# Two-layer recurrent attention: new order times for the nodes inside a tile and near the layer ends, and other reload counts

## The chip, the cores and the metric

The kernel runs on one core of a Trainium2 chip. The metric is the device time of one execution in microseconds: 1611.34 us before, the median of three runs (1610.76 to 1618.56).

## The reference

The input x has 2048 rows of 512 bf16 numbers. Two blocks, A and B, are applied in turn, and the pair twice over with the same weights ("two layers"):

```python
    x = x + _A_ref(_layernorm(x, axis=-1), A_mem0, A_Wq, A_Wk, A_Wv, A_Wo, A_seg_len)
    x = x + _B_ref(_layernorm(x, axis=-1), B_wqkv, B_wo)
```

and the same two lines again. A is attention in 64 segments of 32 rows, one after the other. Each segment puts 8 memory rows in front of its 32 rows, projects these 40 rows to queries, keys and values of 32 heads of 128, takes a masked softmax over the 40 rows and projects back with Wo. The first 8 rows of the outcome are the memory of the next segment; the others are the output rows:

```python
            h = jnp.concatenate([mem, xs], axis=1)
            q = jnp.einsum('btd,dhe->bhte', h, Wq)
...
            o = jnp.einsum('bhte,hed->btd', o, Wo)
            mem = o[:, :M, :].copy()
```

So the 64 segments of a layer are a chain: no K, Q or V of a segment's memory rows can be projected before the segment before is out. B is linear attention over all 2048 rows with 32 heads of 16: phi of keys and queries, the sums kv and z over all rows, then a division and a projection. B's sums need all rows of A, and the second layer's A needs B's outcome.

## The kernel before, in words

All four A weights (4 MB each) stay in SBUF. The kernel walks 64 steps a layer, one per segment; four steps share a tile of 128 rows, so there are 16 tiles a layer, 32 in all. In the text, tile 16 is the first of layer 1, and step 25 is the second step of the seventh tile of a layer. Most matmuls use 32 columns of TensorE, four side by side on the four column groups ("x4" in the timeline).

The work of a step is recorded as nodes by `_Prog.add` (L649): each has a function, what it reads and writes, and a key (layer, step, name, number). Nodes of one step, by name:

- kq0, kq1: project K and Q of half of the heads (L1138, matmuls at L1157 with a weight load and L1053 without), then evict (L937 on ScalarE, L938 on VectorE) and transpose (L1175). v: project the values.
- mem0, mem1: attention of the memory rows, half of the heads each (L1237): scores (L1258, L1264), Exp (L1275), two mask multiplies on VectorE (L1285), the sum matmuls (L1065), Ln and Exp for the reciprocal (L1294, L1296), the product with the values (L1065), a multiply (L1307).
- out: eight matmuls with Wo (L1400), two evictions. next: picks the memory rows (L1424), whose eviction writes the next step's input. Then the next kq0 can start. This loop is the recurrence.
- x: attention of the 32 new rows (L1312), which the next step's out takes up, so it fills TensorE while the recurrence waits.
- res: adds the output rows to y (L1435) and moves them by GpSimd's DMAs (L953) into the rows' place in dx; each fourth step also the "left" rows (the last 8 rows of each segment) with eight DMAs, and then the row add x += dx (L1474). Two DMAs of every step and eight of each fourth have about 0.5 us each on GpSimd.
- bi (b_in, L1545): once a tile, B's first half for the rows that are done: bn_stats (L1097), bn_aggr, two small ScalarE steps, the normalising row (L1103), transposes (L1111), an eviction, and the products for K, V and Q of B with phi. In layer 0 these are full-width 128-column matmuls (`whole`, L1049); in layer 1 they are 32-column ones (`tiled`, L1057 to L1066).
- prep, left0, left1, leftv, lefts: normalisation and projections for the next tile. In layer 1, bo (`b_out`, L1642) gives the next tile's rows from layer 0's B. At the layers' ends: bm (`b_mid`), bl (last `b_out`), spin (matmuls that compute nothing, L1069).

**What sets the order.** The order is written into the program: `schedule()` (L698) gives each node a time by `when()` (L579), sorts all nodes by it, and each engine issues its nodes in this order. The same sort picks the eight PSUM banks, and a letter behind the time picks the engine of an eviction that either engine could do ("a" ScalarE, "v" VectorE):

```python
    own = _OWN.get((layer, step, name), ())
    if k < len(own) and own[k] is not None:
        t, eng = own[k]
    else:
        n, o, table = _PERIOD[layer]
        t, eng = table[name][step % 4][k]
        t += o + n * (step // 4)
```

The times serve only as sort keys; no engine waits for a clock. OWN (L187) has own times for nodes of the first and last steps of a layer; all other tiles take theirs from PERIOD (L19), one table of four steps for each layer, repeated every 44,811 (layer 0) or 47,442 (layer 1). So all tiles 3 to 13 of layer 0 have one order, and tiles 18 to 29 another. `finalize()` (L735) then works out which semaphore waits are needed; a later order may need more or fewer of them.

FRESH (L1130) and the third number of some SPIN entries (L1068) say how many weight loads are issued that the matmul could do without: in the value projection the second part repeats the same weights as the first, and the first `(FRESH + g) // 4` of its matmuls in step g of a tile load them again all the same. PEld in the profile is these loads and all others.

In a steady tile of layer 0, TensorE's program has 1536 matmuls, 1269 loads and 11 waits, 2816 instructions; in layer 1, 1664, 1398 and 10, 3072. Both are multiples of 256.

Of the kernel before, what the change touches and what calls it, by code (L numbers as in the profile page):

```python
# [19 lines left out]
    0: (44811, 12575, {  # L20
# [4 lines left out]
            0: '13110 13623 13859 13975 15568a 16359 16126a 16539',  # L25
            1: '25411 26062 26347 26877 27130v 27885 26918a 27828',
            2: '37244 37328 37706 38196 38237v 39335 38569a 38761',
            3: '46334 46412 46663 46947 47259a 47283 47040v 47538',
        },
        'kq1': {  # L30
            0: '13353 14813 15519 15623 16502a 16799 17302a 18507',
            1: '27317 27535 27794 27900 28953a 29844 28921a 29499',
            2: '38227 38383 38402 39545 39901a 40319 39946v 40115',
            3: '46952 47061 47181 47186 47861a 48996 48101v 48997',
        },
        'v': {
            0: '17492 17691 18869 18940 20511a 21964v',
            1: '27961 28639 28667 29491 30125a 31273a',
            2: '40039 40052 40430 40622 42339v 43144a',
            3: '47627 48767 49623 50288 50598a 52349v',  # L40
        },
        'ql': {
            0: '15578v 15115v',
            1: '17461v 26861v',
            2: '38451a 37269v',
            3: '46898a 43786v',
        },
        'mem0': {
            0: '16546 16829 17294 17722 17785 18016 18583 21138 21803 22217',
            1: '28936 29458 29710 29934 30400 30773 31025 31760 31385 33035',  # L50
            2: '39583 39632 40375 40378 41630 42130 42645 42774 42871 42913',
            3: '47989 48336 48416 49298 49214 51527 52026 52221 51908 52564',
        },
        'mem1': {
            0: '18585 18761 20500 21528 21516 21884 21908 22571 22489 22811',
            1: '29565 29979 30292 31154 31139 32247 33262 33833 33659 33946',
            2: '40730 40943 42442 42507 42731 42909 43420 43710 43574 44077',
            3: '49723 49762 49955 51484 51262 51932 52684 52852 52517 53969',
        },
        'out': {  # L60
            0: '22634 22646 22723 22911 23010 23518 23814 23993 24202a 24185a',
            1: '34034 34103 34175 34442 34686 35087 35287 35328 35887a 35715a',
            2: '43410 43727 43813 44632 44797 44941 45160 45262 45405a 45620a',
            3: '52679 52859 53388 53737 54082 54749 54845 55140 55959a 56101a',
        },
        'next': {
            0: '24849 24871 25273a',
            1: '36147 36448 37154a',
            2: '45618 45634 45742v',
            3: '56912 57244 57340a',  # L70
        },
        'res': {
            0: '24394 25027 25086 14340 14734 14783 16191 16354 17003 17419 18155 19251a 19806a 19967 21627 22615 21487 23944 21934 20248 20479 24471 28189',
            1: '37622 42461 40621',
            2: '46643 49596 51348',
            3: '56350 59264 64311',
        },
        'bi': {
            2: '28195 28607 29504 29672 29909 30351 32430 30430v 31577 31585 31911 32074 37050 37706 38060 64732 66227 69129 69420 69916a 70219 69486 80150 71185 64667 66976 69466 69753 70445 70925 71377 76228',
# [8 lines left out]
            2: '1858 14289 22297 27278 30922 32637 34676v 41100a 36482v 36690v 34762v',  # L88
        },
        'left0': {  # L90
            2: '35441 35565 36649 37230 38164v 45925 41246a 44765',
        },
        'left1': {
            2: '42823 42990 45458 45659 46883a 56541 49015a 57506',
# [1643 lines left out]
```

## Time and profile before

| what | value |
|---|---|
| median of 3 runs | 1611.34 us |
| the profiled execution | 1611.15 us |
| its span | 1609.4 us |
| around the span | 1.75 us |
| granted TensorE clock, mean | 0.998 |
| VectorE evictions (L938) | 576 at 545 ns |
| ScalarE evictions (L937, arena) | 1140 at 488 ns |
| DMAs of GpSimd into dx | 504, issued in 511 ns each, landing after 1.6 and 1.9 us |
| GpSimd busy | 326.8 us |

The profile's engines are PE (TensorE's matmuls), PEld (its weight loads, which overlap PE), DVE (VectorE), ACT (ScalarE), POOL (GpSimd). Matmuls are piped and their ends are modelled, so PE counts as busy in some gaps too. The start takes 43.6 us, of which the first 36 wait for the weights: the transfer of Wv lands 33.8 us after its issue. The last tile of layer 0, with B's middle behind it, takes 71.7 us (747.66 to 819.38), the first two of layer 1 take 44.6 and 49.6, the tile before the last 48.1 (1485.5 to 1533.6).

A row of the waits reads: the engine and line that waited, behind the arrow what it waited for, then the total us, how often, and the longest. A row of the timeline reads: start in us from the span's start, duration, engine, line, operation, output and inputs with their shapes, how many in a row were put together, and in brackets the wait ahead of it.

### The profile page before, as it was taken

How to read it: one execution, taken by the hardware profiler on the slowest of the kernel's cores; microseconds unless marked ns; L12 is line 12 of the kernel's file. 1: busy time of each engine (PE TensorE's matmuls, PEld its weight loads, DVE VectorE, ACT ScalarE, POOL GpSimd, SP SyncE). 2: the span in 40 equal slices, each digit the busy share in tenths (PEclk: the TensorE clock that was granted, in tenths of full speed). 3: DMA queues.
4: the chain of work that ended last, by engine and by line, in shares of the span. 5: the costliest groups of instructions: out<-in, count | busy, mean ns of one | idle time of the engine just before them, and what ended most of it. 6: DMA issues, size and time to landing. Idle time of an engine off the chain costs nothing.

```text
span 1609.4 us, 104163 instructions
## 1 busy us (share of the span) xinstructions
PE 1544.0 (96%) x52074; PEld 882.0 (55%) x43376; DVE 1221.6 (76%) x3899; ACT 1100.0 (68%) x3178; POOL 326.8 (20%) x660
## 2 busy tenths in 40 slices
PE   5899999999999999999999999999999999999997
PEld 1455555555555555555545655556556555555554
DVE  3777777887777787777677778777787877877777
ACT  1567776776776776776467777777777777776665
POOL 2022221122222112222201221222221222221120
PEclk9999999999999999999999999999999999999999
DMA  9300000000000000000000000000000000000013
GB/s 381 104 14 16 14 17 10 16 17 17 17 14 17 10 17 16 17 17 17 25 8 11 17 20 20 20 14 17 21 17 20 21 20 11 21 17 22 24 43 130
DMA packets 35079, 50.96 MB, mean 32 GB/s; under 512 B 13624, under 2 KB 28784, under 8 KB 33104
## 3 DMA queue, kind: packets, MB, share of 16 engines
q0 software_dynamic: 21744, 19.78, 4.3%
q1 hardware_dynamic: 12736, 24.38, 4.1%
q8 instruction: 374, 6.13, 1.6%
q14 instruction: 65, 0.53, 0.1%
q10 hardware_dynamic: 160, 0.14, 0.0%
HBM read 29.63 MB, written 10.49 MB: 25 GB/s over the span
## 4 chain that ended last, share of the span: by engine, by line
PE 85%; DVE 5%; ACT 5%; DMA 2%; issue 1%; POOL 0%; DVEq 0%; SPq 0%
PE pb L1157 27%; PE pb L1053 22%; PE pb L1400 17%; PE pb L1065 11%; ACT arena_sb L937 3%; PE pb L1049 3%; PE pb L1424 2%; DMA Wq_sb<-in_A_Wq_dram 2%; PE pb L1258 2%; DVE arena_sb L938 1%; PE pb L1338 1%; PE pb L1111 1%; DVE st_sb L1097 1%; DMA dx_sb<-y_sb 1%; DVE Wq_sb L1679 1%
## 5 line engine op out<-in xcount | busy, mean ns | idle before, releaser
L937 ACT ACTIVATE arena_sb<-pb 128x512 bf16<-128x512 f32 (+5 forms) x1140 | 521.0, 488 | 273.5 <-PE pb L1053 165.2
L953 POOL DMA_DIRECT2D dx_sb<-y_sb x504 | 254.6, 511 | 1047.7 <-DVE y_sb L1435 822.3
L1157 PE MATMUL pb<-Wk_sb,arena_sb 128*32 128x512 bf16 x4096 | 408.5, 379 | 3.0 <-DVE arena_sb L938 1.4
L1053 PE MATMUL pb<-Wq_sb,arena_sb 128*32 128x512 bf16 x4096 | 408.1, 379 | 0.0
L938 DVE CAST arena_sb<-pb 128x512 bf16<-128x512 f32 (+3 forms) x576 | 311.5, 545 | 110.9 <-PE pb L1053 57.9
L1400 PE MATMUL pb<-Wo_sb,arena_sb 128*32 128x256 bf16 x10368 | 345.3, 273 | 4.3 <-DVE arena_sb L1307 1.7
L1065 PE MATMUL pb<-arena_sb 128*32 128x128 bf16 (+2 forms) x12528 | 321.7, 216 | 4.2 <-ACT arena_sb L937 1.5
L1065 PEld LDWEIGHTS pb<-arena_sb 128*32 128x32 bf16 x12528 | 227.7, 96 | 138.1 <-issue 28.5
L1175 DVE STREAM_TRANSPOSE arena_sb<-arena_sb 128x256 f32<-128x256 f32 x640 | 260.9, 429 | 42.8 <-ACT arena_sb L937 36.6
L1400 PEld LDWEIGHTS pb<-Wo_sb,arena_sb 128*32 128x32 bf16 x10368 | 263.1, 96 | 50.6 <-issue 15.7
L1157 PE MATMUL pb<-Wv_sb,arena_sb 128*32 128x512 bf16 x3248 | 279.6, 378 | 1.1 <-DVE arena_sb L938 1.1
L1157 PEld LDWEIGHTS pb<-Wk_sb,arena_sb 128*32 128x32 bf16 x4096 | 119.4, 96 | 237.5 <-issue 186.2
L1053 PE MATMUL pb<-Wv_sb,arena_sb 128*32 128x512 bf16 x1872 | 202.8, 378 | 0.0
L937 ACT ACTIVATE arena_sb<-arena_sb 32x256 bf16<-32x256 bf16 (+1 forms) x414 | 159.6, 386 | 31.3 <-DVE arena_sb L1345 21.4
L1157 PEld LDWEIGHTS pb<-Wv_sb,arena_sb 128*32 128x32 bf16 x3248 | 95.9, 96 | 73.6 <-issue 19.2
L937 ACT ACTIVATE outW_sb<-pb 128x128 fp32r<-128x128 f32 x317 | 70.3, 273 | 89.2 <-PE pb L1400 86.2
L1307 DVE TENSOR_TENSOR arena_sb<-pb,arena_sb 128x128 bf16<-128x128 f32 x252 | 73.1, 290 | 50.5 <-PE pb L1400 17.2
L1157 PE MATMUL pb<-Wq_sb,arena_sb 128*32 128x512 bf16 x1024 | 101.6, 378 | 4.5 <-DMA Wq_sb<-in_A_Wq_dram 3.4
L1275 ACT ACTIVATE arena_sb<-pb 128x192 bf16<-128x192 f32 (+1 forms) x256 | 83.9, 328 | 31.2 <-PE pb L1258 12.7
L1435 DVE TENSOR_TENSOR y_sb<-pb,outW_sb 64x256 bf16<-64x256 f32 x158 | 65.8, 417 | 47.6 <-ACT outW_sb L937 44.2
L1053 PE MATMUL pb<-Wk_sb,arena_sb 128*32 128x512 bf16 x1024 | 101.7, 378 | 0.0
L1285 DVE TENSOR_TENSOR arena_sb<-arena_sb 128x128 bf16<-128x128 bf16 x504 | 89.0, 215 | 15.9 <-ACT arena_sb L1275 14.1
(109 smaller groups left out, 1793.0 us busy)
## 6 DMA issues: line engine op xcount, KB each, us to landing
Wk_sb<-in_A_Wk_dram SPq DMA_DIRECT2D x1, 4096.0 KB, 13.2
Wq_sb<-in_A_Wq_dram SPq DMA_DIRECT2D x1, 4096.0 KB, 24.3
Wv_sb<-in_A_Wv_dram SPq DMA_DIRECT2D x1, 4096.0 KB, 33.8
Wo_sb<-in_A_Wo_dram SPq DMA_DIRECT2D x16, 256.0 KB, 7.3
xs_scratch<-x_sb POOLq DMA_DIRECT2D x32, 128.0 KB, 2.0
pq_scratch<-arena_sb POOLq DMA_DIRECT2D x32, 128.0 KB, 2.9
dx_sb<-y_sb POOLq DMA_DIRECT2D x252, 12.0 KB, 1.6
dx_sb<-y_sb POOLq DMA_DIRECT2D x252, 4.0 KB, 1.9
```

The lines of the kernel that those rows point to most:

```text
L937: return e.activation(o() if callable(o) else o, i() if callable(i) else i, ACTF.Copy)
L938: return e.tensor_copy(o() if callable(o) else o, i() if callable(i) else i)
L953: add(eng, lambda e: e.dma_start(o, i), 0.55 if eng == "pool" else 0.4, reads=reads, writes=writes, dsem="%s%d" % (kind, k), lat=lat + (0. ...
L1053: return pe.add_instruction(mybir.InstMatmult(name=nc.get_next_instruction_name(), engine=mybir.EngineType.PE, ins=[pe.lower_ap(x), pe.low ...
L1065: r = pe.matmul(o[q], w[:, q], x, start=start, stop=stop, skip_group_check=True, tile_position=(0, 32 * j))
L1157: r = pe.matmul(o, blk[:, c, :], w, start=(c == 0), stop=(c == 3), tile_position=(0, 32 * j))
L1175: add("dve", lambda v: v.transpose(dst, src(img[:, k, :].bitcast(F32))), 0.445, reads=[("img", k)], writes=[dkey])
L1275: add("act", lambda a: a.activation(PQ[:, r2, b, 0:nq], tl.f32()[:, 0:nq], ACTF.Exp, scale=SCALE), c_act(nq), tiles=[tl], writes=[("PQ", r ...
L1285: add("dve", lambda v, a=a, p_=p_, w_=w_: v.tensor_tensor(wide(Pm[:, k, a, :]), p_.unsqueeze(2).to_broadcast([128, 4, 4, 8]), w_, ALU.mult ...
L1307: add("dve", lambda v: v.tensor_tensor(oTb[:, s % NO, 16 * b:16 * b + 16, 0:8], pv.f32()[:, 0:128].rearrange("p (n q) -> p n q", q=8), Rm[ ...
L1400: r = pe.matmul(tl.f32()[32 * j:32 * j + 32, 0:256], oT[:, 4 * hh + n, :], Wo_sb[:, 8 * n + hh, 256 * d:256 * d + 256], start=(hh == 0 and ...
L1435: add("dve", lambda v: v.tensor_tensor(y_sb[0:64, k, :], tl.f32()[0:64, 0:256], outW[64:128, w, :].bitcast(F32), ALU.add), c_dve(256), rea ...
```

## The change

No arithmetic changes. Almost every number of PERIOD and OWN does, and with them the order of nodes on every engine, the PSUM banks and the engine of many evictions; the two periods stay 44,811 and 47,442. Only relative order counts, so a shift of a whole table means nothing by itself. FRESH goes from 21 and 22 to 15 and 21 reloaded weights a tile (layers 0 and 1), and three SPIN entries load more or fewer weights again. In the changed program TensorE has the same 51,113 matmuls, 89 loads fewer and 84 wait instructions more; ScalarE has 34 instructions more and VectorE 34 fewer; GpSimd and SyncE keep theirs. A steady tile of layer 0 has 1536 matmuls, 1263 loads and 17 waits; one of layer 1 has 1664, 1397 and 11: again 2816 and 3072. A core of the diff, with the mem, res and bi rows of layer 0 that the text speaks of:

```diff
 PERIOD = {
-    0: (44811, 12575, {
+    0: (44811, 18084, {
...
         'mem1': {
...
-            1: '29565 29979 30292 31154 31139 32247 33262 33833 33659 33946',
+            1: '21770 21821 23523 24566 23897 25358 25373 25412 25370 26163',
...
         'res': {
...
-            0: '24394 25027 25086 14340 14734 14783 16191 16354 17003 17419 18155 19251a 19806a 19967 21627 22615 21487 23944 21934 20248 20479 24471 28189',
+            0: '16185 19379 21611 10728 11160 11606 11854 11856 12697 12749 12840 13857a 14265a 14789 15054 16464 16352 15143 17517 17857 18390 20872 23421',
...
         'bi': {
-            2: '28195 28607 29504 29672 29909 30351 32430 30430v 31577 31585 31911 32074 37050 37706 38060 64732 66227 69129 69420 69916a 70219 69486 80150 71185 64667 66976 69466 69753 70445 70925 71377 76228',
+            2: '23702 24471 24872 24945 25865 26463 32232 29485v 33953 33965 34004 34019 37178 38888 39017 49910 50024 60490 61903 61918a 68888 62000 71533 63097 60387 66932 66971 68576 72238 74046 74055 80677',
...
-    SPIN = {(0, 0): (24, 256, 46), (1, 0): (12,), (1, 1): (22, 256, 55), (0, 2): (5,), (0, 3): (7,), (0, 4): (30, 512, 42)}
+    SPIN = {(0, 0): (24, 256, 72), (1, 0): (12,), (1, 1): (22, 256, 84), (0, 2): (5,), (0, 3): (7,), (0, 4): (30, 512, 10)}
...
-        FRESH = {0: 21, 1: 22}
+        FRESH = {0: 15, 1: 21}
```

In these rows the last number of 'res' in step 0 is the row add x += dx, and the first of 'bi' is its bn_stats; the fourth and fifth of 'mem1' are the mask multiplies of the second half and the sixth its sum matmuls.

## The prediction

> **What bounds the kernel now.** I read the page's busy rows first, then the chain that ended last, then each stage's windows, then what TensorE waits for. The first two:
>
> ```profile
> PE 1544.0 (96%) x52074; PEld 882.0 (55%) x43376; DVE 1221.6 (76%) x3899; ACT 1100.0 (68%) x3178; POOL 326.8 (20%) x660
> ...
> PE 85%; DVE 5%; ACT 5%; DMA 2%; issue 1%; POOL 0%; DVEq 0%; SPq 0%
> ```
>
> TensorE holds the end: 85% of the chain. VectorE and ScalarE are each 5%, 161 us together of a span of 1609.4. No edit here takes matmul columns away, so the question is how much of the time that is not columns the new order gives back. The windows (us, then busy us and count of PE, PEld, DVE, ACT, POOL; granted clock; DMA) are layer 0's tiles 3 to 14, tile 6, tile 7, a tile of layer 1, and the end:
>
> ```profile
> 183.37:747.66 564.29, 555.59 (x18450) 316.48 (x15280) 437.32 (x1446) 396.88 (x1161) 118.20 (x232) 1.00 0.06 16
> 323.83:370.54 46.71, 46.19 (x1535) 26.49 (x1270) 36.31 (x121) 33.23 (x98) 9.71 (x20) 1.00 0.06 15
> 370.54:418.85 48.31, 46.49 (x1534) 25.81 (x1269) 36.27 (x121) 33.06 (x98) 9.68 (x20) 1.00 0.05 15
> 1056.32:1103.87 47.55, 46.68 (x1668) 27.65 (x1398) 37.54 (x120) 34.62 (x103) 10.28 (x21) 1.00 0.07 18
> 1533.60:1609.40 75.80, 64.11 (x2050) 36.62 (x1835) 55.56 (x137) 47.17 (x117) 13.27 (x26) 0.99 0.28 92
> ```
>
> A layer-0 tile takes about 46.7 us and one of layer 1 47.55, and they repeat: 12 and 13 such tiles are 1,180 us of the 1609. "Busy" overstates TensorE, since the modelled ends of piped matmuls run on over a gap. Adding for each matmul of a tile the shortest distance from its start to the next start that the timeline shows gives 44.37 and 45.61 us. So about 2.34 us a tile of layer 0, and 1.94 in layer 1, are waits and changes between full-width and 32-column matmuls. This is all that an order can give back there: 12 x 2.34 + 13 x 1.94 = 53 us. Who is waited for:
>
> ```profile
> PE pb L1065 <- DVE arena_sb L1285: 13.4, 31, 2.5
> PE pb L1111 <- DVE arena_sb L1103: 10.9, 4, 8.9
> PE pb L1049 <- DVE arena_sb L938: 4.7, 14, 0.8
> ```
>
> Row 1 is the sum matmul of the memory rows waiting for its two mask multiplies: 9.8 of its 13.4 us lie in layer 1's steady tiles, 0.75 us each. Row 3 is layer 0's b_in waiting for the normalised rows (12 of 14 times in steady tiles). Row 2 sits where the layers start. The timeline of the first shows its making:
>
> ```profile
> 1063.12 0.42 DVE L1474 TENSOR_TENSOR x_sb<-x_sb,dx_sb 128x512 bf16<-128x512 bf16 x1
> 1063.57 0.69 DVE L1097 BATCH_NORM_STATS2 st_sb<-x_sb 128x6 f32<-128x512 bf16 x1
> 1064.18 0.34 DVE L1285 TENSOR_TENSOR arena_sb<-arena_sb 128x128 bf16<-128x128 bf16 x2
> 1064.58 0.24 PE L1065 MATMUL pb<-arena_sb,one_sb 128*32 128x128 bf16 x4 [0.60 <-DVE arena_sb L1285]
> ```
>
> The row add and bn_stats stand on VectorE between the two halves' multiplies: 1.1 us ahead of two that take 0.34, and TensorE stops 0.60.
>
> **The change part by part.** *Work.* The matmuls are the same 51,113. The reloads that go (6 and 1 a tile, L1130) hide: the K matmuls that load and the Q matmuls of the same shape that reuse weights both have a mean of 379 ns in the groups. I take 0; since PEld lies wholly beside PE, a bound is 6 x 96 ns (mean load) = 0.6 us a tile of gain if it did not, 7 in all; loads missing elsewhere can't add time. 34 evictions go from VectorE (545 ns by the L938 row) to ScalarE (488): 18 us off one, 17 onto the other, both under 80% busy, so 0 by itself; its worth is in the waits below. The work of POOL and SP keeps its count.
>
> *Layer 0's steady tiles.* For each matmul that waits on an eviction I added up, from the trace's durations, the shortest way to it from the matmul before (matmul, 0.22 us until the eviction starts, its duration, 0.055 us to the waiting matmul), and set against it the TensorE work ordered between. Where the way is longer, the tile is late by the rest. Before: b_in's first matmul (0.93 of way, 0.71 of cover) 0.21; its sums behind phi (1.09 against 0.77) 0.32; the pick of the memory rows 0.125; the second product of memory attention 0.10; out 0.09; smaller ones. Run in order, 0.85 us a tile. After, the first two have ample cover and what is left is the next step's first K/Q matmul, 0.53 against 0.285, and 0.03: 0.28. That is -0.57. The rest of the measured 1.3 us of waits, about 0.45, is queueing on the two helper engines, which I can only bound: the new order puts the row add and bn_stats between the halves' multiplies here too, as layer 1 has them, and layer 1 pays 0.6 to 0.8 for it at 0.81 of cover. Here the cover is longer; I take 0.15 more (bounds 0 and 0.8). Two more mode changes a tile (10 to 12):
>
> ```profile
> 370.90 0.23 PE L1053 MATMUL pb<-arena_sb,one_sb 128*32 128x128 bf16 x4
> 371.06 0.40 PE L1049 MATMUL pb<-arena_sb 128*128 128x128 bf16 x4
> 371.39 0.28 PE L1065 MATMUL pb<-arena_sb 128*32 128x128 bf16 x12
> ```
>
> Each group of four 32-column matmuls has 0.053 us of columns (128 of them at 2.4 a ns, the pitch of the long runs), but the full-width matmul starts 0.16 later: about 0.10 a change. [...] I take the row, since the distance is what the next matmul paid. Sum for a tile: -0.57 + 0.15 + 0.20 = -0.22, and -0.1 more because edges within 0.25 us of late fall from 30 to 19, and each such edge turns helper jitter into a stop: about -0.3 (bounds -0.8 and +0.5). Twelve tiles: **-3.6** (-9.6 to +6).
>
> *Layer 1's steady tiles.* The same sum goes from 0.76 to 0.56. K/Q 0.24 to 0.105; the sums 0.18 to 0.12; out's first product stays, 0.43 to 0.46. VectorE keeps the row add and bn_stats between the halves, so row 1 of the waits stays; moving evictions to ScalarE frees VectorE (44.0 to 40.8 us of durations a tile) and loads ScalarE (39.9 to 42.4), where a value eviction now stands ahead of the second half. I take -0.15 of the -0.20 (bounds -0.6 and +0.6): **-2** for 13 tiles. The eight small DMAs of the left rows are issued behind an add that moves about 1 us later (from -1.74 to -0.77 us of TensorE work in the step), and their reader, the row add, stays (6.18 to 6.12): slack for them falls from about 1.6 to 0.6 us, still hidden (ten issues at the 0.51 us row, plus the 1.9 us landing row).
>
> *The start.* TensorE stops until the value weights land (near 35.6 us). Before, 14.5 us of its work is ordered ahead of that; after, 16.2, and the first out stands behind 20.2 us of work instead of 23.6. About 1.7 to 3.4 are won if the first steps keep up; they run at 10.3 to 10.8 us by their own chains and can give some back. I take **-3** (-5 to +1). *Tiles 14 to 17*: waits +0.35, ten more mode changes in tile 15 (18 to 28) at 0.10: **+1.4** (0 to +4). *Tile 30 and the end*: the same sums, 8.4 to 7.0, less what queueing takes back: **-1** (-3 to +1).
>
> Sum: -3 - 3.6 + 1.4 - 2 - 1 = -8.2 on the profiled 1611.15 (1609.4 of span and 1.75 around it), which stands 0.2 under the median: **1603 us**.
>
> **The rivals.** *Nothing measurable.* Waits move rather than go: the two helpers together have 72 of 93 us filled in a tile, my ways leave out their queues, and in layer 1 queueing was larger (1.94 - 0.76 = 1.2) than what the ways explain. If queueing grows by 0.57 in layer 0 and 0.2 in layer 1, what is left is +3.1 for mode changes and -3 at the start: 1611. For it: VectorE's row add stays where it is in layer 1. *More.* If layer 0's queueing falls with the near-late edges (-0.8 a tile) and layer 1 gains 0.4: -9.6 - 5.2 - 1.6 = 1595. *Slower.* The second half's sums in layer 0 stop behind the row add and bn_stats for the whole of these two rows, 0.42 + 0.69 = 1.1 us, in place of the 0.15 that I took: a layer-0 tile is then -0.57 + 1.1 + 0.20 = +0.73, twelve 8.8. The same delay in the first steps takes the start's gain, layer 1 gives nothing, and with +1.4 and -1 this is 1620. It decides once the two rows reach VectorE less than 1.1 us before the second half's exponentials end. The DMAs are not it: tile 7's one late landing cost 1.7 us, but slack is left. *It does nothing* in layer 1: as said, that tile's worst wait is kept.
>
> **How the numbers follow.** The forecast has 0.54 (of it 0.30 under 1603.3), more gain 0.15, nothing 0.13, slower 0.18. About 0.5%, 8 us, is what a measurement of this kernel can tell from no change: faster 0.45, same 0.37, slower 0.18. The range leaves out 0.07 below and 0.09 above: 1592 to 1621. With both signs in it, the forecast's own range is 1597 to 1609.
>
> **What would show it.** In the profile after: steady layer-0 tiles of 46.4 us (right) or 47.4 (the slower rival); the wait of L1049 for L938 gone; L1065 for L1285 still about 10 us in layer 1, and under 3 in layer 0 (8 or more: the slower rival); layer-1 tiles of 47.4; the end of tile 0 some 3 us earlier; tile 15 a us longer; PEld busy down by about 9 us with no change of PE's. A wait on dx_sb in the chain, or tiles that differ from each other, would make me wrong, as would a layer-1 tile that changes by over 0.6 us.

## The result, and the profile after

The changed kernel takes 1607.62 us (median; 1604.27 to 1611.62), the kernel before, measured beside it, 1612.94. The ratio is 0.9969 with an interval of 0.9962 to 0.9975: 5.0 us, or 0.3%, faster, where 8.2 had been forecast. The kernel before was measured beside each experiment too and had medians of 1612.9 to 1617.6, so kernels are compared by their ratios to it. The two profiled executions differ by 4.0 us (1611.15 and 1607.17), their spans by 4.2.

The page after has these busy rows and this chain:

```profile
PE 1550.3 (97%) x52121; PEld 880.0 (55%) x43287; DVE 1218.7 (76%) x3865; ACT 1101.0 (69%) x3212; POOL 324.9 (20%) x660
...
PE 88%; DVE 5%; ACT 2%; DMA 2%; issue 1%; POOL 0%; SPq 0%; DVEq 0%; ACTq 0%
```

ScalarE's share of the chain falls from 5% to 2% though it has 34 instructions more, TensorE's rises from 85% to 88%: less of the chain runs through ScalarE. PEld falls by 2.0 us, not by 9. The windows of the stages, with the columns as before (the bounds are the first K/Q matmul of step 4, step 8 and step 56 of layer 0, then of steps 0, 8 and 56 of layer 1; the stretch 82.83 to 129.49 is left out):

```profile
0.00:82.83 82.83, 59.81 (x1693) 24.98 (x1270) 42.88 (x137) 31.38 (x92) 13.38 (x50) 1.00 0.63 236
129.49:688.81 559.32, 558.78 (x18484) 317.68 (x15201) 453.89 (x1458) 383.52 (x1152) 115.98 (x228) 1.00 0.06 15
688.81:801.30 112.49, 109.69 (x3379) 62.26 (x2816) 83.83 (x259) 70.54 (x194) 26.74 (x52) 1.00 0.07 21
801.30:900.32 99.02, 95.94 (x3177) 51.13 (x2598) 74.42 (x237) 65.89 (x191) 12.79 (x25) 1.00 0.05 13
900.32:1470.70 570.38, 560.05 (x19983) 331.17 (x16769) 425.68 (x1381) 435.70 (x1273) 122.68 (x240) 1.00 0.07 18
1470.70:1605.20 134.50, 120.66 (x3993) 69.20 (x3457) 102.36 (x288) 84.13 (x221) 24.06 (x47) 0.99 0.19 61
```

The same stages of the kernel before, cut at the same matmuls, and the forecast's terms:

| stage | before, us | after, us | difference | forecast |
|---|---|---|---|---|
| start to step 4 | 81.33 | 82.83 | +1.5 | -3 (start) |
| step 4 to step 8 | 46.34 | 46.66 | +0.3 | in the start |
| layer 0, steps 8 to 56 (12 tiles) | 562.87 | 559.32 | -3.55 | -3.6 |
| layer 0's last two tiles, B's middle | 116.73 | 112.49 | -4.2 | +1.4 together |
| layer 1, steps 0 to 8 | 95.22 | 99.02 | +3.8 | (tiles 14 to 17) |
| layer 1, steps 8 to 56 (12 tiles) | 571.79 | 570.38 | -1.4 | -2 |
| the rest | 135.12 | 134.50 | -0.6 | -1 |
| sum | 1609.4 | 1605.2 | -4.2 | -8.2 |

The rows of -4.2 and +3.8 belong together: the first of them has 74 matmuls fewer than before and the second 37 more, so work has moved across the mark, and what is left of both is -0.4. Tile by tile, the steady tiles of layer 0 took 46.5 to 47.2 us and now 46.36 to 46.85. Tile 7 stands out: 48.52, now 46.85. So 1.7 of the 3.55 us are one event in one tile, and the eleven others gained 0.17 on the mean. In layer 1 the tile stays at 47.5 us.

One pair of profiles is not exact for the short stages. Five kernels below begin like one of the two, so there are four profiles of the old start and three of the new. The first matmul on the value weights came anywhere from 35.5 to 37.7 us, in both. From it to step 4, the old start took 45.40 to 45.45 us and the new one 46.5 to 47.05, so this part is 1.1 to 1.6 us longer. The whole to step 4 took 81.27 to 83.11 us in the old start and 82.09 to 83.50 in the new; there the difference between the kernels is hardly larger than the scatter.

What TensorE waits for, over the whole span (engine, line, behind the arrow what came last, then total us, times, longest):

```profile
PE pb L1067 <- DVE arena_sb L1287: 12.8, 20, 2.5
PE pb L1113 <- DVE arena_sb L1105: 10.3, 3, 9.1
...
PE pb L1426 <- ACT outW_sb L939: 2.2, 7, 0.4
...
PE pb L1055 <- issue: 1.2, 1, 1.2
```

The b_in row (L1049 for L938, 4.7 us) is gone, and L1067 for L1287 is nearly the size it was. In the window of layer 0's steady tiles (176.48 to 734.95 us) the waits have no row at all; before, b_in's matmuls alone had 5.6 us there:

```profile
PE pb L1049 <- DVE arena_sb L938: 3.7, 12, 0.3
PE pb L1049 <- issue: 1.9, 12, 0.2
```

These two rows mislead. The trace of the kernel before has 465 records of L1049's matmuls for 512 weight loads, and each of these waits stands at the second matmul of a group, 0.23 us behind the load of a first one that has no record. A kernel below with the same order in layer 0 and all 512 records (the new tables in layer 1 alone) has no such row in its tiles: there the 1.9 us are no wait, and of the 3.7 only about 0.15 us a tile is one (see the gaps below). In layer 1 the row stays; its making, in the timeline:

```profile
1108.16 0.42 DVE L1476 TENSOR_TENSOR x_sb<-x_sb,dx_sb 128x512 bf16<-128x512 bf16 x1
1108.61 0.69 DVE L1099 BATCH_NORM_STATS2 st_sb<-x_sb 128x6 f32<-128x512 bf16 x1
1109.22 0.34 DVE L1287 TENSOR_TENSOR arena_sb<-arena_sb 128x128 bf16<-128x128 bf16 x2
1109.62 0.24 PE L1067 MATMUL pb<-arena_sb,one_sb 128*32 128x128 bf16 x4 [0.63 <-DVE arena_sb L1287]
```

It is the picture of before to a few hundredths. And one stop is new, in the second step; nothing that the profile shows released the matmul behind it:

```profile
50.34 0.39 PE L1159 MATMUL pb<-Wk_sb,arena_sb 128*32 128x512 bf16 x4
51.96 0.38 PE L1055 MATMUL pb<-Wq_sb,arena_sb 128*32 128x512 bf16 x4 [1.23 <-issue]
```

The change has two parts, the order and the reload counts. The forecast gave the gain to the order (small waits in layer 0's tiles) and counted the reloads at 0. The experiments set against this: that the gain is the reloads' own; that the counts have a price by where they put TensorE's instructions; that in layer 1 another engine comes late once VectorE doesn't; and that the start is lost by its own chain. The expectations use letters for theories, and the text under each says in words which reading held.

### The profile page after: what moved, and what is told of

The parts are those of the page before. It is cut to its first block, busy times and chain, and to the rows that moved or that the text cites. A ratio compares the mean times of both kernels' runs of the same rounds, so it can differ in the third digit from the quotient of the medians.

```text
span 1605.2 us, 104159 instructions
## 1 busy us (share of the span) xinstructions
PE 1550.3 (97%) x52121; PEld 880.0 (55%) x43287; DVE 1218.7 (76%) x3865; ACT 1101.0 (69%) x3212; POOL 324.9 (20%) x660
## 3 DMA queue, kind: packets, MB, share of 16 engines
q8 instruction: 374, 6.13, 1.6%
## 4 chain that ended last, share of the span: by engine, by line
PE 88%; DVE 5%; ACT 2%; DMA 2%; issue 1%; POOL 0%; SPq 0%; DVEq 0%; ACTq 0%
PE pb L1159 27%; PE pb L1055 23%; PE pb L1402 18%; PE pb L1067 11%; PE pb L1051 3%; DMA Wv_sb<-in_A_Wv_dram 2%; ACT arena_sb L939 2%; PE pb L1260 1%; PE pb L1426 1%; PE pb L1113 1%; PE pb L1340 1%; DVE st_sb L1099 1%; DVE arena_sb L940 1%; DVE arena_sb L1287 1%; DVE Wq_sb L1681 0%
## 5 line engine op out<-in xcount | busy, mean ns | idle before, releaser
L939 ACT ACTIVATE arena_sb<-pb 128x512 bf16<-128x512 f32 (+5 forms) x1234 | 556.2, 485 | 276.9 <-PE pb L1055 182.2
L940 DVE CAST arena_sb<-pb 128x512 bf16<-128x512 f32 (+3 forms) x510 | 275.7, 544 | 103.4 <-PE pb L1055 66.5
L1067 PE MATMUL pb<-arena_sb 128*32 128x128 bf16 (+2 forms) x12528 | 326.8, 216 | 5.0 <-DVE arena_sb L1606 2.0
L1067 PEld LDWEIGHTS pb<-arena_sb 128*32 128x32 bf16 x12528 | 227.2, 96 | 130.9 <-issue 39.0
L1159 PE MATMUL pb<-Wv_sb,arena_sb 128*32 128x512 bf16 x3136 | 281.0, 378 | 1.3 <-DMA Wv_sb<-in_A_Wv_dram 0.7
L1402 PEld LDWEIGHTS pb<-Wo_sb,arena_sb 128*32 128x32 bf16 x10368 | 259.1, 97 | 35.8 <-issue 9.2
L1055 PE MATMUL pb<-Wv_sb,arena_sb 128*32 128x512 bf16 x1984 | 210.3, 378 | 0.0
L939 ACT ACTIVATE arena_sb<-arena_sb 32x256 bf16<-32x256 bf16 (+1 forms) x377 | 143.2, 380 | 14.5 <-DVE arena_sb L1347 4.6
L1159 PEld LDWEIGHTS pb<-Wv_sb,arena_sb 128*32 128x32 bf16 x3136 | 90.0, 96 | 79.2 <-issue 25.1
L1287 DVE TENSOR_TENSOR arena_sb<-arena_sb 128x128 bf16<-128x128 bf16 x504 | 91.8, 216 | 29.5 <-ACT arena_sb L1277 27.7
L1277 ACT ACTIVATE arena_sb<-pb 128x192 bf16<-128x192 f32 (+1 forms) x256 | 85.0, 333 | 41.6 <-PE pb L1260 38.1
L940 DVE COPY arena_sb<-arena_sb 32x256 bf16<-32x256 bf16 (+1 forms) x391 | 79.7, 207 | 9.1
```

The costliest lines, as they stand in the source:

```text
L939: return e.activation(o() if callable(o) else o, i() if callable(i) else i, ACTF.Copy)
L940: return e.tensor_copy(o() if callable(o) else o, i() if callable(i) else i)
L1055: return pe.add_instruction(mybir.InstMatmult(name=nc.get_next_instruction_name(), engine=mybir.EngineType.PE, ins=[pe.lower_ap(x), pe.low ...
L1067: r = pe.matmul(o[q], w[:, q], x, start=start, stop=stop, skip_group_check=True, tile_position=(0, 32 * j))
L1159: r = pe.matmul(o, blk[:, c, :], w, start=(c == 0), stop=(c == 3), tile_position=(0, 32 * j))
L1277: add("act", lambda a: a.activation(PQ[:, r2, b, 0:nq], tl.f32()[:, 0:nq], ACTF.Exp, scale=SCALE), c_act(nq), tiles=[tl], writes=[("PQ", r ...
```

## The two parts of the change apart

**The new order with the old counts.** The changed kernel, with the counts of before:

```diff
-    SPIN = {(0, 0): (24, 256, 72), (1, 0): (12,), (1, 1): (22, 256, 84), (0, 2): (5,), (0, 3): (7,), (0, 4): (30, 512, 10)}
+    SPIN = {(0, 0): (24, 256, 46), (1, 0): (12,), (1, 1): (22, 256, 55), (0, 2): (5,), (0, 3): (7,), (0, 4): (30, 512, 42)}
-        FRESH = {0: 15, 1: 21}
+        FRESH = {0: 21, 1: 22}
```

> The new order with the old reload counts (21 and 22 a tile, the old SPIN entries), so a tile is no longer 2816 or 3072 instructions of TensorE. Theory A, the order carries the change and the counts nothing: the time of the changed kernel, 1607.6 within 1 us. Theory B, the counts carry it: 1611 or more.

Measured: 1664.83 us, 1.0291 [1.0269, 1.0313] of the kernel before. The second reading held, and by far more than its 1611: the counts carry it, but not by their work. The same matmuls in the same order, with 89 weight loads more, are 52 us slower than the changed kernel (1.0291 against 0.9969), 0.58 us for each load, whose mean duration is 0.096. Its waits:

```profile
PE pb L1402 <- issue: 12.6, 32, 0.9
PE pb L1067 <- issue: 11.5, 16, 2.7
...
PE pb L1159 <- issue: 8.6, 19, 1.0
PE pb L1055 <- issue: 3.9, 8, 0.9
```

"issue" says that nothing in the profile released the engine. These stops have a place, though. I numbered TensorE's instructions (matmuls, loads and waits) in program order, each load just ahead of its matmul. All 77 waits that the profile puts down to "issue", 37.1 us together, stand in front of an instruction whose number leaves 193 or 194 when divided by 256. The page has a row that fits, of the changed kernel here:

```profile
q8 instruction: 374, 6.13, 1.6%
```

374 packets are 6.13 MB, 16 KB each, and the 95,838 instructions of TensorE in the trace are 374 blocks of 256: each packet is one block of TensorE's program. The packets of this queue show how it runs. In the kernel with the old counts, a block's packet starts mostly 0.6 to 1.3 us after TensorE's first matmul of the block before it and takes 0.9 to 1.4. In none of the four kernels that I went through block by block (before, changed, this one, and the one with shifted borders) does a block's first matmul come sooner than 1.2 us after the landing. One case in this kernel: a block entered at 324.75, the next block's packet late, from 326.50 to 327.45, that block's first matmul at 328.80 after a wait of 0.54. A tile's mean is 4.2 us a block (46.5 us for 11), but its dense stretches of short matmuls pass 256 instructions in 2.7 to 3.4. Where the border falls in the tile decides whether a dense stretch is a block by itself or is shared between two.

A short block alone is not the cause. Of the blocks that took under 3.1 us (from 60 us on, the stop not counted), 68 of 83 end in a stop of 0.09 us or more in this kernel, and 2 of 52 in the kernel before. What differs is the next block's packet: with the stops it starts 0.83 us (median) after the short block's first matmul, in the kernel before 0.24 us ahead of it. Why it starts sooner at some places is not shown.

So this is what the counts do. A steady tile of the changed kernel has 2816 instructions, eleven blocks exactly, so the borders fall at the same places in each tile. With the old FRESH it has 2822, and the borders move by 6 places from tile to tile. In layer 0 the tiles here take 47.3 to 49.3 us instead of 46.4 to 46.9, in layer 1 (3073 instead of 3072) 49.5 to 50.8.

In the right place a crossing mostly costs nothing that shows: of the 120 crossings in the changed kernel from 183 to 690 us (layer 0's steady tiles), 116 show no stop of 0.09 us or more. The worst stop of the kernel above is 2.7 (at the end of its first step).

**The old order with the new counts.** The kernel before, with FRESH and SPIN of the changed one:

```diff
-        FRESH = {0: 21, 1: 22}
+        FRESH = {0: 15, 1: 21}
```

> The kernel before with the new reload counts (15 and 21, the new SPIN entries): the fourth corner of order by counts. With the counts 6 and 1 instructions a tile short of a multiple of 256, Theory D (the place of the block boundary in the tile decides) gives a drift through bad places as in the new order with the old counts: 1640 to 1670. Rival, fewer reloads are themselves a gain: 1612 or less.

Measured: 1639.95 us, 1.0156 [1.0138, 1.0174], a loss, as the reading by place had it. Tiles of 2810 and 3071, borders that move: layer 0's take 47.1 to 48.3, layer 1's 48.2 to 50.9, and the new row of its waits is again without a releaser:

```profile
PE pb L1065 <- issue: 8.9, 17, 1.9
```

So the two parts do not add up; each is a loss of 1.6% or 2.9% alone:

| | old counts | new counts |
|---|---|---|
| old order | 1 | 1.0156 |
| new order | 1.0291 | 0.9969 |

**The borders shifted, with nothing else changed.** In the changed kernel, reloads in the spin stretches of the start and of the first layer's end, where TensorE computes nothing that is used, move every border by 106 places in layer 0 and by 126 in layer 1. The tiles keep their 2816 and 3072:

```diff
-    SPIN = {(0, 0): (24, 256, 72), (1, 0): (12,), (1, 1): (22, 256, 84), (0, 2): (5,), (0, 3): (7,), (0, 4): (30, 512, 10)}
+    SPIN = {(0, 0): (24, 256, 92), (1, 0): (12,), (1, 1): (22, 256, 84), (0, 2): (5,), (0, 3): (7,), (0, 4): (30, 512, 116)}
```

> The changed kernel with more reloads in three SPIN entries alone (116, 92 and 84 in place of 10, 72 and 84), so that every later instruction of TensorE stands 106 (layer 0) and 126 (layer 1) places further; a tile stays 2816 or 3072 instructions. Theory D, a matmul at a fixed place modulo 256 waits for the next block of instructions, and costs where TensorE passes 256 instructions faster than a block lands: in the changed kernel's own timeline the shifted places lie round denser stretches, 1 to 2 us more a tile, so 1630 to 1660. Theory E, only a tile that is no multiple of 256 is harmful: 1607.6.

Measured: 1675.23 us, 1.0385 [1.0369, 1.0401], more than the 1630 to 1660 of the reading by place. Borders that stand still are not enough; the place itself decides. The same eleven tiles of layer 1, the changed kernel first, then this one:

```profile
947.69:1470.70 523.01, 513.52 (x18318) 303.56 (x15372) 390.19 (x1266) 399.41 (x1167) 112.46 (x220) 1.00 0.07 18
```

```profile
975.97:1538.77 562.80, 525.52 (x18318) 321.72 (x15372) 389.20 (x1265) 402.07 (x1167) 112.47 (x220) 1.00 0.06 17
```

18318 matmuls and 15372 loads in both, the clock at 1.00, the helpers' busy times within 3 us, and 39.8 us more. The waits of this kernel name where:

```profile
PE pb L1067 <- issue: 29.6, 45, 1.5
...
PE pb L1402 <- issue: 9.4, 28, 0.7
PE pb L1426 <- issue: 8.3, 14, 1.0
```

Over the whole span, the stops of 0.09 us or more in front of the first matmul behind a border come to the sums below. A stop is here the distance between two starts less the time of the first one's columns (0.213 us for 512, the pitch at which groups of four follow each other in long runs).

| kernel | span, us | crossings that stop | us |
|---|---|---|---|
| before | 1609.4 | 11 | 3.3 |
| changed | 1605.2 | 25 | 8.7 |
| new order, old counts | 1669.2 | 124 | 60 |
| old order, new counts | 1638.8 | 64 | 30 |
| changed, borders shifted | 1677.9 | 129 | 71 |
| changed, b_in of layer 0 in 32 columns (below) | 1619.3 | 50 | 25 |
| changed, one group less (below) | 1611.3 | 31 | 14.5 |

The stops make up most of what the spans differ by: 52 of 64 us for the old counts, 62 of 73 for the shifted borders, 26 of 29 for the old order. So the counts are no saving of loads; they hold the new order's borders where they cost little. And the borders cost the changed kernel 5.4 us more than the old kernel's: 1.6 more in the start (the stop of 1.23 above is one) and 1.9 more at the end.

## Layer 0's tiles

**The new tables in layer 0's steady steps alone.** The kernel before, with steps 10 to 57 of layer 0 sorted by the new tables, the rest by the old, FRESH 15 and 22, and SPIN set so that the borders stay in place. Times of two tables do not fit together everywhere, so in this and the two other kernels with two tables the sort also holds a node back until all that it needs is placed and a bank is free. In outline:

```diff
-        n, o, table = _PERIOD[layer]
+        n, o, table = (_PERIOD2 if layer == 0 and 10 <= step < 58 else _PERIOD)[layer]
...
-        FRESH = {0: 21, 1: 22}
+        FRESH = {0: 15, 1: 22}
```

> The kernel before with the new order in layer 0's steps 10 to 57 alone (15 reloads a tile there). Theory A: its steady tiles take 46.4 to 46.5 us in place of 46.6 to 47.2, in all 2 to 3.5 us off 1612.9, so 1609.4 to 1610.9. Theory C, that what went there was only a late dx transfer in one profiled execution (1.7 us in tile 7) and not a wait of every tile: within 0.7 us of the kernel before.

Measured: 1624.27 us, 1.0040 [1.0027, 1.0053], slower, where 2 to 3.5 us less had been expected. The tiles between the joints show the gain: eleven of them (steps 12 to 56) take 513.78 us against 515.65 before. But the two joints cost more: steps 8 to 12 take 54.69 us (about 47 without a joint) and 56 to 60 take 51.96 (48.1), since neither order has the work of the other's next tile done when it begins. A cut in the middle of a program measures its joints too; only the windows between them say what was asked.

Over all profiles, the same eleven tiles without tile 7 take 46.70 to 46.86 us each in the old order (four kernels) and 46.54 to 46.69 in the new (six): 0.15 a tile. To see where, I took the same distances less columns, of over 0.04 us, tile by tile without tile 7: for the old order from the kernel with the new tables in layer 1 alone, whose trace has all records, for the new from the changed kernel.

| us a tile | old order | new order |
|---|---|---|
| changes between full-width and 32-column matmuls | ten, 0.97 | twelve, 1.19 |
| wait ahead of a full-width group of b_in | 0.15 | none |
| next and its pick, K/Q, out in the third step | 0.41 | none |
| ahead of b_in's transposes | none | 0.18 |
| others | 0.19 | 0.12 |
| sum | 1.72 | 1.49 |

A change shows as 0.09 to 0.12 us wherever it stands, in both orders: the 0.10 that the forecast took. The K/Q wait that the forecast saw left in the new order (0.245) is not there: of the four steps of a tile, the first K/Q matmul has a gap of 0.12 in one, behind a full-width matmul, and at most 0.02 in the others. What came instead is the 0.18 at the transposes. The row add and bn_stats now stand between the halves here too, VectorE of the changed kernel in tile 8:

```profile
425.84 0.42 DVE L1476 TENSOR_TENSOR x_sb<-x_sb,dx_sb 128x512 bf16<-128x512 bf16 x1
426.30 0.70 DVE L1099 BATCH_NORM_STATS2 st_sb<-x_sb 128x6 f32<-128x512 bf16 x1
427.34 0.23 DVE L1287 TENSOR_TENSOR arena_sb<-arena_sb 128x128 bf16<-128x128 bf16 x1 [0.35 <-ACT arena_sb L1277]
```

The "slower" rival rested on a stop behind these two rows; here the exponentials of the second half come late enough for VectorE to be through with both.

**b_in of layer 0 in 32-column matmuls.** With no full-width matmuls, the mode changes go. Each such matmul becomes four, and the reloads (FRESH, SPIN and a few of K and Q) are set so that a tile is whole blocks again (twelve). The main lines:

```diff
-        FRESH = {0: 15, 1: 21}
+        FRESH = {0: 64, 1: 21}
+        AGAIN = {0: 15, 1: 0}
...
-        wide, mode = (whole, 1) if layer == 0 else (tiled, 0)
+        wide, mode = tiled, 0
```

> The changed kernel with layer 0's b_in in 32-column matmuls as in layer 1, so that no mode changes are left in a tile; 192 instructions more a tile, and 64 more reloads that make it 3072. If a change of mode costs what the gaps round each of the six groups show (0.22 us a group, 14 tiles): 18 us less, 1590. If the twelfth block of instructions takes some 1 us a tile of it back: 1604. Rival, a change of mode is free and the gaps are modelled ends: 1607.6 or more.

Measured: 1619.51 us, 1.0036 [1.0022, 1.0051]; tiles of 46.7 to 47.8. Neither 1590 nor 1604, so the third reading's number, but not its reason: the gaps around the groups did go. Stops at blocks' borders (9.8 us instead of 0.9 in the eleven tiles, with a block more in each) and old waits came in, as its waits in layer 0's tiles show:

```profile
PE pb L1403 <- issue: 6.3, 15, 1.1
PE pb L1067 <- DVE arena_sb L1288: 2.6, 11, 0.6
```

Less the border stops, it comes out some 0.3 us a tile under the changed kernel, an estimate from the two profiles (46.22 against 46.50). So of the 1.19 us of changes 0.3 were won: a gap that goes lets other waits show, and the worth of one change is not isolated by this.

**One group less.** In the changed kernel, two products of b_in join the next group, five groups a tile in place of six:

```diff
-... 60387 66932 66971 68576 72238 ...
+... 60387 68560 68570 68576 72238 ...
```

> The changed kernel with two of layer 0's b_in query products (numbers 25 and 26) moved next to 27 and the value product of keys (20), past two 32-column steps: five groups of full-width matmuls a tile in place of six, so ten changes of mode in place of twelve, and the same instructions. By the forecast's 0.10 a change: 0.2 us a tile, 11 tiles, 2.2 less, 1605.4. If changes are free or the gap only moves: 1607.6.

Measured: 1613.00 us, 0.9985 [0.9974, 0.9997], so not better than the changed kernel's 0.9969. The group's two changes (0.19) are gone and a wait of 0.17 has come at the second product. Tiles stay at 46.4 to 46.9. The rest of the difference lies outside layer 0's tiles, in border stops (14.5 us over the span, against 8.7).

**What holds up tile 7.** In the old order, a dx transfer of GpSimd follows a pause that has no releaser, and the row add waits for it. The transfer itself is slow as well: 3.1 us from issue to landing, where the median is 1.6. The kernel before, GpSimd then VectorE:

```profile
377.03 0.51 POOL L953 DMA_DIRECT2D dx_sb<-y_sb  x1 [1.73 <-issue]
```

```profile
380.21 0.43 DVE L1474 TENSOR_TENSOR x_sb<-x_sb,dx_sb 128x512 bf16<-128x512 bf16 x1 [1.81 <-DMA dx_sb<-y_sb]
```

If GpSimd too had a border of blocks, 39 more of its instructions would move the pause. A setup memset of the kernel before, cut into 40:

```diff
-            pool(lambda p: p.memset(wm_sb[:, :, :], 1.0), ["wm"])
+            def ones(p):
+                for i in range(40):
+                    r = p.memset(wm_sb[:, i // 8, 4 * (i % 8):4 * (i % 8) + 4], 1.0)
+                return r
+            pool(ones, ["wm"])
```

> The kernel before with one GpSimd memset of the setup cut into 40 small ones, which puts every later GpSimd instruction 39 places further and nothing else. In the kernel before GpSimd stops 1.73 us ahead of the last dx transfer of layer 0's tile 7, the row add waits 1.81 us for it, and this tile takes 48.5 in place of 46.6. Theory: this stop is GpSimd's own next block of instructions; then it moves to where nobody waits, tile 7 takes 46.7, and the time falls by up to 1.9 us. Rival, the transfer is late for another reason of tile 7: 48.5 stays.

Measured: 1614.58 us, 0.9998 [0.9987, 1.0010]. The pause stays at the same transfer, and tile 7 at 48.59:

```profile
378.65 0.51 POOL L953 DMA_DIRECT2D dx_sb<-y_sb  x1 [1.73 <-issue]
```

So the rival held: the pause doesn't go by GpSimd's instructions. Does it go by its transfers? One more of them, tile 0's store issued twice:

```diff
-        x_move(xs_view[t], x_sb[:, slot(t), :], slot(t), [("x", slot(t))], [("xs", t)], "dxs")
+        for _ in range(2 if layer == 0 and t == 0 else 1):
+            P.count = 6
+            x_move(xs_view[t], x_sb[:, slot(t), :], slot(t), [("x", slot(t))], [("xs", t)], "dxs")
```

> The kernel before with the 128-row store of tile 0's rows issued twice by GpSimd (same data), one transfer more early in the program and the same instructions on the other engines. The stop of GpSimd ahead of tile 7's last dx transfer stayed at that transfer when 39 instructions were put before it, so the theory now: it comes after a certain amount of transfers (some 75 by GpSimd, or so many rows). Then it stands one transfer or 128 rows earlier, and tile 7 takes 46.6 to 47.5 in place of 48.5, the whole up to 1.9 us less. Rival, it belongs to this transfer or this moment: 48.5 stays.

Measured: 1616.55 us, 0.9991 [0.9980, 1.0003]; the pause comes one transfer of the program earlier, again in front of GpSimd's 132nd, the row add still waits 2.18 us, and tile 7 takes 48.71. This fits a count of transfers, but the later pauses of this run don't: those that stood in front of the 205th, 281st and 400th transfer now stand one number further, at the same transfers of the program. The cause stays open. In the changed kernel, GpSimd then VectorE:

```profile
377.48 0.53 POOL L955 DMA_DIRECT2D dx_sb<-y_sb  x1 [1.52 <-issue]
```

```profile
379.19 0.43 DVE L1476 TENSOR_TENSOR x_sb<-x_sb,dx_sb 128x512 bf16<-128x512 bf16 x1
```

The pause is still there, and the row add behind it waits no more than 0.11 us: the transfer landed in 1.6 us. That is not the order alone. In two later profiles with the same order in these steps (a shorter bn_stats, and the scores first, both below) the same transfer took 3.4 and 3.5 us, the row add waited 1.8 and 1.9, and tile 7 took 47.63 and 47.73. In four profiles, the changed kernel's among them, tile 7 took about 46.85. The old order had 48.52 to 48.89 in all four of its own. So, as an estimate, about 0.9 us in this tile goes with the order, and the other 0.8 with the execution.

Tile 14 gained 1.9 us; no run was made for that one.

## Layer 1's tiles

**The new tables in layer 1's steady steps alone.** As above, with `layer == 1 and 8 <= step < 58`, and one SPIN count 55 to 57 to hold the borders.

> The kernel before with the new order in layer 1's steps 8 to 57 alone (21 reloads a tile there). The tiles of the two profiles are alike (47.55 and 47.56), so Theory A: 1612.9 less 0 to 1.5 us. If the moved evictions are worth what the forecast said (0.15 a tile): 1610.9.

Measured: 1621.67 us, 1.0031 [1.0019, 1.0044]. Neither reading's time came, since the joint at steps 8 to 12 takes 52.89 us; the tiles behind it take 47.5 to 48.1, as in both kernels. Over all profiles, eleven of layer 1's tiles take 524.1 to 525.9 us in the old order and 523.0 to 525.7 in the new: as they stand, hardly a gain. Less the border stops, though, they part: 523.8 to 524.4 in four profiles of the old order, 521.9 to 522.5 in five of the new. By this estimate the order won some 0.17 us a tile; the border stops of the eleven tiles came to 1.2 to 3.4 us in the new order and 0.4 to 1.5 in the old, which takes most of it back.

**A shorter bn_stats.** Is VectorE what layer 1's sums wait for? In layer 1, bn_stats of b_in reads 64 of the 512 columns, which leaves out most of the rows' statistics:

```diff
-        add("dve", lambda v: v.bn_stats(st[:, 0:6], x), c_dve(512), reads=[xk], writes=[("st", k)])
+        add("dve", lambda v: v.bn_stats(st[:, 0:6], x[:, 0:cols]), c_dve(512), reads=[xk], writes=[("st", k)])
...
-        tl = layernorm(t, busy)
+        tl = layernorm(t, busy, 512 if layer == 0 else 64)
```

> The changed kernel with bn_stats of layer 1's b_in over 64 of the 512 columns, which leaves out most of the row statistics and takes about 0.5 us of VectorE from between the two halves' mask multiplies. Theory F, the forecast's reading that the row add and bn_stats are what the sum matmul waits for (0.84 us a tile): the whole 0.5 is won, 13 tiles, 1601. Theory G, the second half's exponentials on ScalarE end 0.06 us before VectorE is free, in the changed kernel's timeline, so they are late next: 0.2 a tile, 1605.

Measured: 1607.76 us, 0.9962 [0.9950, 0.9975]: the changed kernel's ratio, so neither reading's gain, and tiles of 47.4 to 48.0. The timeline at the same place:

```profile
1111.97 0.23 DVE L1099 BATCH_NORM_STATS2 st_sb<-x_sb 128x6 f32<-128x64 bf16 x1
1112.03 0.33 ACT L1277 ACTIVATE arena_sb<-pb 128x192 bf16<-128x192 f32 x1
1112.39 0.36 DVE L1287 TENSOR_TENSOR arena_sb<-arena_sb 128x128 bf16<-128x128 bf16 x2 [0.19 <-ACT arena_sb L1277]
...
1112.80 0.24 PE L1067 MATMUL pb<-arena_sb,one_sb 128*32 128x128 bf16 x4 [0.45 <-DVE arena_sb L1287]
```

bn_stats is 0.46 us shorter, and the mask multiplies start only 0.19 sooner against their surroundings, for now they wait for the exponentials on ScalarE (L1277), which end at 1112.36. Of a wait of 0.63 bn_stats owns some 0.2; ScalarE is right behind. And the 0.2 does not reach the tile's end: the second product then waits 0.18 for ScalarE's value eviction, and out starts 2.04 us behind the row add in both kernels.

## The start

**The old order in the first steps.** The changed kernel with layer 0's steps below 10 by the old tables (and one SPIN count 10 to 4 to hold the borders).

> The changed kernel with the old order in layer 0's steps up to 9. In the profiles the new start is 1.8 us late at step 8. If that is lost for good: 1605.8. Rival, the old start only borrows work from later steps and gives it back: 1607.6.

Measured: 1620.55 us, 1.0013 [1.0000, 1.0025]. The joint at steps 8 to 12 takes 54.70 us and covers what was asked: inconclusive.

**The memory scores ahead of the value projection.** In the changed kernel's first step the memory rows' scores are ordered behind the value projection, and that waits for Wv: the first matmul of mem0 is at 40.58 us, before at 34.30. So their times were moved forward, with the sort that holds nodes back (above) and one SPIN count 10 to 12:

```diff
-    (0, 0, 'mem0'): '26620 26648 27794 30401 30262 30677 31029 31338 30789 31852',
-    (0, 0, 'mem1'): '26592 29206 30254 30851 31351 31627 31979 32080 31739 32760',
+    (0, 0, 'mem0'): '22600 22610 22700 24600 24610 26010 26300 26500 28700 28800',
+    (0, 0, 'mem1'): '26592 26650 28210 28580 28590 29000 29300 29400 29500 30000',
```

> The changed kernel with the first step's memory scores, exponentials and multiplies ahead of most of the value projection, as in the kernel before. Theory: the new start loses since this chain stands behind the value weights' landing; then the first out comes 1.5 to 2 us earlier and the end with it, 1606. Rival, later steps of the start are bound by their own chain or fetches and nothing reaches the end: 1607.6.

Measured: 1609.05 us, 0.9967 [0.9954, 0.9979], as the changed kernel's 0.9969; step 4 begins at 82.76 instead of 82.83. But the run does not answer its question: the first scores came at 40.24 us, hardly sooner than 40.58, and the first out at 47.51, later than the changed kernel's 45.82, after a wait of 1.49 for VectorE.

What the two profiles show of the start is this. The first out comes 2.45 us later in the changed kernel (45.82 against 43.37), yet the second step begins at the same time, the kernel before first:

```profile
49.56 0.40 PE L1157 MATMUL pb<-Wk_sb,arena_sb 128*32 128x512 bf16 x4 [0.19 <-DVE arena_sb L938]
```

```profile
49.47 0.40 PE L1159 MATMUL pb<-Wk_sb,arena_sb 128*32 128x512 bf16 x4
```

So a late first out was not the loss here. Then comes the stop of 1.23 us at a block's border. That block's packet started at 49.51, three microseconds after the border before it (46.49). The two other profiles with this start have a stop of 1.3 and 1.4 us at a border one block earlier, in the first step's out (the short bn_stats, one group less); the four with the old start have none over 0.5 up to step 4. This is nearly all of the 1.1 to 1.6 us by which the new start is longer. Why these packets come late is not shown.

## Where the prediction was right, and where it was not

- **The bound and the sign** held: TensorE's share of the chain is 88%, and what was won is waits in layer 0.
- **Layer 0's steady tiles**, -3.6 forecast, -3.55 measured: the number fits in part by luck. 1.7 are tile 7's late transfer, which the forecast mentions only as no danger and of which some 0.8 go with the execution; the eleven others give 0.15 to 0.17 each where it had 0.3. Its terms: two more changes between widths, 0.20 forecast, 0.22 found. Over the whole span the two traces have 163 changes before and 195 after; 32 more at the 0.09 to 0.12 found are 2.9 to 3.8 us, where "Nothing measurable" has +3.1. Old waits of 0.85 in all, of which about 0.56 show as gaps; the row that the forecast read for b_in (L1049 for L938) is mostly missing records, with a wait of about 0.15 behind it for 0.21, and this did go. The 0.15 for a stop behind the row add and bn_stats did not come, nor did the 0.245 left at K/Q; 0.18 ahead of b_in's transposes came instead.
- **Layer 1**, -2 forecast, -1.4 in the two profiles: "row 1 of the waits stays" was right, and less the border stops the order's gain is about the size forecast. The reading that the row add and bn_stats make that wait was right for 0.2 of its 0.63 to 0.84 us where bn_stats was cut; ScalarE's exponentials are behind for the rest.
- **The start**, -3 forecast, 1.5 to 1.8 lost in the two profiles, is the step that failed. "After, 16.2, and the first out stands behind 20.2 us of work instead of 23.6" counts cover as work of TensorE; but in the new order the scores stand behind work that waits for Wv, so the first out came 2.45 us later, not earlier. The second step began no later for it, so nothing was won and nothing lost by then; the loss is a block border's stop of 1.2 to 1.4, of which the forecast had nothing. By the two profiles this is 4.8 us off the sum. The layers' change went the other way, -0.4 for +1.4, since work moved across it, and layer 1 and the end gave 1.0 less: together the 4.0 that the forecast is off in the spans.
- **The reloads.** "I take 0 ... loads missing elsewhere can't add time" is right for this kernel by its counts only. With the order and the old counts the time is 52 us more. Loads carry place as well as work; both kernels hold the tile at a multiple of 256, which the description ahead of the prediction states and the prediction made nothing of.
- **PEld**, -9 forecast, -2.0 measured: 89 loads by their mean of 96 ns overcounts, for four loads lie side by side on the column groups. The row of value loads has 3136 of them in 90.0 us busy, 28.7 ns each; 89 x 28.7 = 2.6.

Not settled: what a change between widths is worth once its gap is gone, the cause of GpSimd's pauses, why a block's packet comes early at some places and late at others, what sets the start of the second step, and how tiles 14 to 17 share their -4.2 and +3.8.

## What to carry to other kernels

When a reorder adds or removes instructions on the bound engine, count them modulo the instruction block (256 here) and look where "issue" waits repeat: some hundred idle weight loads, in the right or the wrong place, are worth 25 to 67 us here, and the whole change won 5. Before a wait is counted as won, find what ends second: taking 0.46 us off VectorE moved the sums by 0.2 and the tile by nothing. Before a wait is counted at all, compare the number of records with the number of weight loads: a missing matmul looks like a wait (465 records for 512 loads here). In a start bound by loads, cost the chain to the first output through each load it stands behind, not the amount of work ahead of it; and test a part of an order only in the windows between its joints.

## What was not expected of the hardware

- TensorE's program comes in packets of 256 instructions, one for each block passed, and in the four kernels gone through a block's first matmul never came sooner than 1.2 us after its packet's landing. Where the packet was late for a short block, TensorE stopped, by up to 2.7 us at once; shifted borders cost 62 us in a program of 1607 (71 less 8.7), and of the changed kernel's 120 crossings in layer 0's steady tiles 116 show no stop of 0.09 us or more.
- In the changed kernel's first two steps, two packets in a row started 3.3 and 3.0 us after the border before them; the median of its 374 packets is 0.55.
- GpSimd pauses 1.5 to 1.9 us between two DMA issues, always in front of its 132nd transfer and at a few later places. In the kernel before, 39 more instructions ahead did not move the first pause, and one more transfer moved that one, but not the later ones, to an earlier place in the program.
- One dx transfer behind that pause took 3.1 us to land in the old order, and 1.6 or 3.4 in different executions of the new.
